# A two-part last output block, earlier loads on GpSimd and a shorter set-up, in a kernel of linear attention and an MLP

## The chip, the cores and the metric

The kernel runs on one core of a Trainium2 chip. The metric is the device time of one execution in microseconds (us). A profiled execution also gives a "span", from the core's first to its last instruction, some 2 us less than the time. Five engines run side by side: PE (TensorE), VectorE (DVE), ScalarE (ACT), GpSimd (POOL) and SyncE (SP).

## The reference, cut to what matters

```python
def _attn_ref(q, k, v, lam):            # q, k, v: 4 x 8 heads x 768 x 64
    for b in range(nb):                 # blocks of the sequence
        intra = einsum(qb, kb) * Dmask  # Dmask = lam ** (i - j) where i >= j, else 0
        intra = einsum(intra, vb)
        inter = einsum(qb * lam_pow, kv_state)
        out[:, :, sl] = intra + inter
        kv_state = lam_block * kv_state + einsum(kb_dec, vb)

def _moe_ref(x, w_in, w_out):           # x: 3072 x 512, made of the attention's output
    h = x @ w_in                        # 512 -> 2048
    g = np.where(h >= 1, h, np.where(h <= -1, 0.0, (h + 1) ** 2 / 4))
    return g @ w_out                    # 2048 -> 512
```

## The kernel before: the parts that matter

The tokens come in 24 chunks of 128. The decay is folded into q and k by tables of exponentials, made from a row of positions. A plan, computed when the kernel is built, gives each engine its order of work. The first six chunks are "plain" (transposed on PE through an identity matrix), and their loads, but for chunk 0's k and q, are issued by POOL, as are the weights, in four quarters each. I call the first product `h` L1 and the second L2.

```python
pos_i = const.tile([128, NCB], I32)
nc.gpsimd.iota(pos_i, pattern=[[C, NCB]], base=-S // 2, channel_multiplier=1)
row_i = const.tile([128, S], I32)                       # S = 768
nc.gpsimd.iota(row_i, pattern=[[1, S]], base=-S // 2, channel_multiplier=0)
ident = const.tile([128, 128], BF16)
make_identity(nc, ident)                                # two instructions on POOL
# ... cut ...
def tabq(i, hp):
    r = row[:, i * C:(i + 2) * C].rearrange("p (a b) -> p a b", b=C)
    nc.scalar.activation(out=tab_q[:, i:i + 2, hp, :], in_=r, func=AF.Exp, scale=ln_t[:, hp:hp + 1])
# ... cut ...
order = [("c", 0), ("c", 1), ("w", 0), ("c", 2), ("w", 1), ("c", 3), ...]    # chunks and weight quarters
# ... cut ...
def f_l2(s, ms, kg):                                    # one 128 x 512 block of the output, 16 products
    if kg == 0:
        py_t[s, ms] = pp_y.tile([128, d_model], F32, name="py", tag="py")
    for ko in range(4 * kg, 4 * kg + 4):
        nc.tensor.matmul(py_t[s, ms], lhsT=gT[s][:, ko, ms * 128:(ms + 1) * 128], rhs=w_out_sb[:, ko, :],
                         start=(ko == 0), stop=(ko == FO - 1))
def f_y(s, ms):
    osb[s, ms] = op.tile([128, d_model], F32, name="osb", tag="osb")
    nc.scalar.copy(out=osb[s, ms], in_=py_t[s, ms])
# ... cut ...
for _ in range(int((t - pe_end - 60) // (216 if t > 8000 else 430))):        # dummy matmuls where the plan sees PE wait
    nc.tensor.matmul(spin, lhsT=idle[:, 0:128], rhs=idle, start=True, stop=True)
```

## Time and profile before

| | before |
|---|---|
| time, median of three runs (lowest to highest) | 216.89 us (216.68 to 216.95) |
| time and span of the profiled execution | 215.84 and 213.8 us |
| first load issued by POOL | 2.17 us |
| first L1 matmul, second run of L1 | 13.12 and 18.29 us |
| last matmul ends, kernel ends | 209.88 and 213.82 us |

### The profile page before, as it was taken

How to read it: one execution, taken by the hardware profiler on the slowest of the kernel's cores; microseconds unless marked ns; L12 is line 12 of the kernel's file. 1: busy time of each engine (PE TensorE's matmuls, PEld its weight loads, DVE VectorE, ACT ScalarE, POOL GpSimd, SP SyncE). 2: the span in 40 equal slices, each digit the busy share in tenths (PEclk: the TensorE clock that was granted, in tenths of full speed). 3: DMA queues.
4: the chain of work that ended last, by engine and by line, in shares of the span. 5: the costliest groups of instructions: out<-in, count | busy, mean ns of one | idle time of the engine just before them, and what ended most of it. 6: DMA issues, size and time to landing. Idle time of an engine off the chain costs nothing.

```text
span 213.8 us, 5674 instructions
## 1 busy us (share of the span) xinstructions
PE 206.2 (96%) x2306; PEld 146.3 (68%) x2306; DVE 160.4 (75%) x238; ACT 150.6 (70%) x305; POOL 118.2 (55%) x150
## 2 busy tenths in 40 slices
PE   7899999999999999999899989999999999999992
PEld 2576988676759886978777767767776776666440
DVE  7627898989998999999999999779658546455100
ACT  6798785398668899699799778776778755444121
POOL 8999726169999799687477863865743000000000
PEclk9999999999999999999999999999999999999999
DMA  5999999999999998978977868888870310111121
GB/s 133 243 241 268 203 260 268 212 217 260 229 265 260 231 234 204 208 173 165 237 200 168 213 140 191 216 159 195 201 169 19 107 49 3 49 49 52 49 88 59
DMA packets 95593, 36.80 MB, mean 172 GB/s; under 512 B 87376, under 2 KB 91472, under 8 KB 95568
## 3 DMA queue, kind: packets, MB, share of 16 engines
q1 hardware_dynamic: 89920, 28.06, 58.0%
q0 software_dynamic: 5504, 8.39, 18.1%
q8 instruction: 18, 0.29, 0.6%
q14 instruction: 7, 0.06, 0.1%
q10 hardware_dynamic: 144, 0.00, 0.0%
HBM read 27.27 MB, written 6.29 MB: 157 GB/s over the span
## 4 chain that ended last, share of the span: by engine, by line
PE 64%; DVE 22%; POOL 5%; issue 3%; DMA 2%; ACT 2%; ACTq 0%; POOLq 0%
PE py L418 30%; PE ph L379 26%; DVE w L397 6%; DVE t L393 4%; DVE gT L412 4%; DVE kq L270 3%; DMA x2f<-in_v_dram 2%; DVE kq L267 2%; DVE sc L342 2%; POOL vn L281 1%; PE pu L318 1%; PE po L362 1%; PE ps L335 1%; PE po L360 1%; POOL x2f L461 1%
## 5 line engine op out<-in xcount | busy, mean ns | idle before, releaser
L379 PE MATMUL ph<-xT,w_in_sb 128*128 128x128 bf16 (+1 forms) x1152 | 97.2, 237 | 0.0
L418 PE MATMUL py<-w_out_sb,gT 128*128 128x512 bf16 x384 | 94.3, 379 | 0.0
L379 PEld LDWEIGHTS <-w_in_sb 128*128 128x128 bf16 x1152 | 80.2, 98 | 11.6 <-DMA w_in_sb<-in_moe_w_in_dram 0.4
L387 ACT ACTIVATE r<-ph,one 128x512 bf16<-128x512 f32 x96 | 65.0, 687 | 32.2 <-PE ph L379 20.3
L284 POOL TENSOR_TENSOR vn<-x2f,tab_k 64x256 bf16<-64x256 f32 x72 | 57.5, 798 | 32.3 <-DMA x2f<-in_v_dram 22.0
L418 PEld LDWEIGHTS <-gT 128*128 128x128 bf16 x384 | 35.2, 98 | 29.7
L393 DVE TENSOR_SCALAR t<-r 128x1024 bf16<-128x1024 bf16 x48 | 29.7, 620 | 19.8 <-ACT r L387 19.6
L412 DVE TENSOR_TENSOR gT<-w,t 128x1024 bf16<-128x1024 bf16 x48 | 39.5, 823 | 1.5
L397 DVE TENSOR_TENSOR w<-r,t 128x1024 bf16<-128x1024 bf16 x48 | 38.9, 811 | 1.2
L321 ACT CAST ubd<-pu 64x256 bf16<-64x256 f32 x76 | 27.7, 365 | 6.1 <-PE pu L318 5.2
L287 POOL COPY vi<-vn 64x512 bf16<-64x512 bf16 x36 | 30.6, 850 | 2.0
L423 ACT COPY osb<-py 128x512 f32<-128x512 f32 x24 | 14.0, 585 | 12.9 <-PE py L418 11.4
L265 ACT CAST kq<-x1f 64x256 bf16<-64x256 f32 x54 | 21.7, 401 | 0.6
L369 ACT CAST xT<-po 128x512 bf16<-128x512 f32 x24 | 14.0, 583 | 4.4 <-PE po L362 2.1
L270 DVE TENSOR_TENSOR kq<-x0f,tab_n 128x512 bf16<-128x512 f32 x18 | 15.1, 836 | 0.2
L342 DVE TENSOR_TENSOR sc<-ps,causal 128x512 bf16<-128x512 f32 x18 | 12.3, 682 | 3.4 <-PE ps L335 3.3
L235 PE MATMUL py<-idle 128*128 128x512 bf16 x34 | 11.5, 462 | 1.2 <-DVE one L120 1.2
L267 DVE TENSOR_TENSOR kq<-x1f 64x256 bf16<-64x256 f32 x18 | 11.7, 652 | 0.6
L362 PE MATMUL po<-sc,vi 128*128 128x64 bf16 x144 | 10.5, 193 | 1.6 <-DVE sc L342 1.5
L318 PEld LDWEIGHTS <-kq 128*128 128x128 bf16 x132 | 7.7, 98 | 4.6
L360 PEld LDWEIGHTS <-ubd 128*128 128x128 bf16 x132 | 8.9, 98 | 2.5 <-issue 1.7
L360 PE MATMUL po<-xq,ubd 128*128 128x64 bf16 x132 | 10.5, 193 | 0.0
(62 smaller groups left out, 127.5 us busy)
## 6 DMA issues: line engine op xcount, KB each, us to landing
out_dram<-osb SPq DMA_DIRECT2D x24, 256.0 KB, 2.3
x1f<-in_k_dram SPq DMA_DIRECT2D x19, 256.0 KB, 3.5
x0f<-in_q_dram SPq DMA_DIRECT2D x19, 256.0 KB, 4.0
x2f<-in_v_dram SPq DMA_DIRECT2D x18, 256.0 KB, 4.1
w_in_sb<-in_moe_w_in_dram POOLq DMA_DIRECT2D x4, 512.0 KB, 7.5
w_out_sb<-in_moe_w_out_dram POOLq DMA_DIRECT2D x4, 512.0 KB, 11.8
x2f<-in_v_dram POOLq DMA_DIRECT2D x6, 256.0 KB, 5.9
x1f<-in_k_dram POOLq DMA_DIRECT2D x5, 256.0 KB, 6.8
```

The costliest lines, as they stand in the source:

```text
L265: nc.scalar.copy(out=o, in_=i)
L270: nc.vector.tensor_tensor(kq[c % NKQ][:, 2 * HP:, :].rearrange("p a (b d) -> p (a b) d", b=2), qkv_ld[c, 0], _bc(tab_n[:, c % NCB, :], 2, ...
L284: nc.gpsimd.tensor_tensor(vn[c % NV][HD[hi], HP * g:HP * g + HP, :], quarter(qkv_ld[c, 2], g, hi), _bc(tab, 2, D), op=AX.mult)
L287: nc.gpsimd.tensor_copy(vi[c % NV][HD[hi], :, HD[hi]], vn[c % NV][HD[hi]])
L321: nc.scalar.copy(out=ubd[(2 * c + j) % NUB][HD[hi], :, HD[hi]], in_=pu[0][HD[hi], :, HD[hi] if c < NCB else HD[0]])
L360: nc.tensor.matmul(po[:, hp, HD[j]], lhsT=ubd[(2 * c + j - 1) % NUB][:, hp, :], rhs=qT[c][:, hp, HD[j]], start=True, stop=False)
L379: nc.tensor.matmul(ph[:, j * m:(j + 1) * m], lhsT=w_in_sb[:, ko, (i + j) * 128:(i + j + 1) * 128], rhs=xT[s][:, ko, p * m:(p + 1) * m], st ...
L387: nc.scalar.activation(out=r_t[grp][:, i, :], in_=ph_t[s, ni, part], func=AF.Relu, bias=one[:, 0:1])
L393: nc.vector.tensor_scalar(t_t[grp], r_t[grp], 0.5, 1.0, op0=AX.mult, op1=AX.min)
L397: nc.vector.tensor_tensor(w_t[grp], r_t[grp], t_t[grp], op=AX.subtract)
L412: nc.vector.tensor_tensor(o, w, t, op=AX.mult)
L418: nc.tensor.matmul(py_t[s, ms], lhsT=gT[s][:, ko, ms * 128:(ms + 1) * 128], rhs=w_out_sb[:, ko, :], start=(ko == 0), stop=(ko == FO - 1))
```

## The change

It has four parts. (1) Set-up: POOL makes a row of 256 positions, not 768; the identity moves to VectorE; the tables of later chunk pairs get their offset as a bias. So POOL's loads start sooner. (2) The plan is told that POOL is free at 1200 ns, not 2250, and orders anew. (3) `WIDE` goes from 4 to 6: the scores of chunks 4 and 5 are made in one step, into two banks. (4) The last output block is computed as 384 and then 128 columns, evicted by two engines and stored in two pieces.

```diff
-    PLAIN, KA, WIDE = 6, 2, 4
+    PLAIN, KA, WIDE = 6, 2, 6
+    CUT = 384
-    row_i = const.tile([128, S], I32)
-    nc.gpsimd.iota(row_i, pattern=[[1, S]], base=-S // 2, channel_multiplier=0)
+    row_i = const.tile([128, 2 * C], I32)
+    nc.gpsimd.iota(row_i, pattern=[[1, 2 * C]], base=-S // 2, channel_multiplier=0)
-    make_identity(nc, ident)
+    nc.vector.tensor_tensor(ident, row[:, 0:128], pos[:, 0:1].to_broadcast([128, 128]), op=AX.is_equal)
-    nc.scalar.copy(out=row[:, 2 * C:], in_=row_i[:, 2 * C:])
+        off = dict(bias=off_q[:, i // 2, hp:hp + 1]) if i else {}
+            nc.scalar.mul(off_q[:, i], ln_t, float(2 * C * i))
... (cut) ...
-            y = pst[c, 1] = wide
+            y = pst[c, 1] = wide if c < 4 else pp_t.tile([128, HP, 128], F32, name="pt", tag="pt")
-            add(("t", c), ..., [..., ("qT", c - 1)], ...)
+            add(("t", c), ..., [..., ("qT", c - 1), ("m", c - 1, 1) if c > 4 else None], ...)
... (cut) ...
+        parts = [(py_t[s, ms][0], slice(0, CUT if last else d_model), range(4 * kg, 4 * kg + 4))]
+        if last and kg == CPS - 1:
+            py_t[s, ms].append(pp_y.tile([128, d_model], F32, name="py", tag="py"))
+            parts.append((py_t[s, ms][1], slice(CUT, d_model), range(FO)))
... (cut) ...
+            nc.vector.tensor_copy(osb[s, ms, 1][:, n:], py_t[s, ms][1][:, n:])
... (cut) ...
-    run_plan({"PE": 5500, "ACT": 4450, "DVE": 4650, "POOL": 2250, "DMA": 2700, "SP": 800})
+    run_plan({"PE": 5500, "ACT": 4450, "DVE": 4650, "POOL": 1200, "DMA": 2700, "SP": 800})
```

More of the change, by code (lines that the diff above doesn't have):

```diff
@@ L5 @@
 from concourse import mybir
-from concourse.masks import make_identity
 from concourse._compat import with_exitstack
@@ L121 @@
     pos = const.tile([128, NCB], F32)
-    row = const.tile([128, S], F32)
+    row = const.tile([128, 2 * C], F32)
     nc.vector.tensor_copy(pos, pos_i)
-    nc.vector.tensor_copy(row[:, 0:2 * C], row_i[:, 0:2 * C])
+    nc.vector.tensor_copy(row, row_i)
+    nc.vector.tensor_tensor(ident, row[:, 0:128], pos[:, 0:1].to_broadcast([128, 128]), op=AX.is_equal)
     late = const.tile([128, 1], F32)
@@ L147, in tabq, with f_off @@
     def tabq(i, hp):
-        r = row[:, i * C:(i + 2) * C].rearrange("p (a b) -> p a b", b=C)
-        nc.scalar.activation(out=tab_q[:, i:i + 2, hp, :], in_=r, func=AF.Exp, scale=ln_t[:, hp:hp + 1])
-    const.tile([128, 8], F32, name="pad1")
+        off = dict(bias=off_q[:, i // 2, hp:hp + 1]) if i else {}
+        nc.scalar.activation(out=tab_q[:, i:i + 2, hp, :], in_=row.rearrange("p (a b) -> p a b", b=C), func=AF.Exp,
+                             scale=ln_t[:, hp:hp + 1], **off)
+    off_q = const.tile([128, NCB // 2, HP], F32)
+    def f_off():
+        for i in range(1, NCB // 2):
+            nc.scalar.mul(off_q[:, i], ln_t, float(2 * C * i))
+    const.tile([128, 52], F32, name="pad1")
     w_in_sb = big.tile([128, KO, d_ff], BF16)
@@ L414, in f_l2 @@
     def f_l2(s, ms, kg):
+        last = (s, ms) == (NST - 1, CPS - 1)
         if kg == 0:
-            py_t[s, ms] = pp_y.tile([128, d_model], F32, name="py", tag="py")
-        for ko in range(4 * kg, 4 * kg + 4):
-            nc.tensor.matmul(py_t[s, ms], lhsT=gT[s][:, ko, ms * 128:(ms + 1) * 128], rhs=w_out_sb[:, ko, :],
-                             start=(ko == 0), stop=(ko == FO - 1))
+            py_t[s, ms] = [pp_y.tile([128, d_model], F32, name="py", tag="py")]
+        parts = [(py_t[s, ms][0], slice(0, CUT if last else d_model), range(4 * kg, 4 * kg + 4))]
+        if last and kg == CPS - 1:
+            py_t[s, ms].append(pp_y.tile([128, d_model], F32, name="py", tag="py"))
+            parts.append((py_t[s, ms][1], slice(CUT, d_model), range(FO)))
+        for t, j, kos in parts:
+            for ko in kos:
+                nc.tensor.matmul(t[:, j], lhsT=gT[s][:, ko, ms * 128:(ms + 1) * 128], rhs=w_out_sb[:, ko, j],
+                                 start=(ko == 0), stop=(ko == FO - 1))
     def f_y(s, ms):
         osb[s, ms] = op.tile([128, d_model], F32, name="osb", tag="osb")
-        nc.scalar.copy(out=osb[s, ms], in_=py_t[s, ms])
+        n = CUT if len(py_t[s, ms]) > 1 else d_model
+        nc.scalar.copy(out=osb[s, ms][:, 0:n], in_=py_t[s, ms][0][:, 0:n])
+        if n < d_model:
+            osb[s, ms, 1] = op.tile([128, d_model], F32, name="osb", tag="osb")
+            nc.vector.tensor_copy(osb[s, ms, 1][:, n:], py_t[s, ms][1][:, n:])
     def f_st(s, ms):
         m0 = s * MS + ms * 128
-        nc.sync.dma_start(out=out[m0:m0 + 128, :], in_=osb[s, ms])
+        n = CUT if len(py_t[s, ms]) > 1 else d_model
+        nc.sync.dma_start(out=out[m0:m0 + 128, 0:n], in_=osb[s, ms][:, 0:n])
+        if n < d_model:
+            nc.sync.dma_start(out=out[m0:m0 + 128, n:], in_=osb[s, ms, 1][:, n:])
     T0, STEP, LEAD = 24000, 1000, 5000
@@ L498 @@
     add(("tabk",), "ACT", 250, lambda: nc.scalar.activation(out=tab_k, in_=arg, func=AF.Exp, scale=-1.0))
+    add(("off",), "ACT", 2 * 230, f_off, [("tab", 0, 3)])
     add(("tabn",), "ACT", 250, lambda: nc.scalar.activation(out=tab_n, in_=arg, func=AF.Exp), [("x", PLAIN - 3)])
@@ L510 @@
         for hp in range(HP) if P and c % 2 == 0 else ():
-            add(("tab", c, hp), "ACT", 410, lambda c=c, hp=hp: tabq(c, hp), [("tab", c, hp - 1), (None, ("kb", 0), ("x", 1))[c // 2]])
+            add(("tab", c, hp), "ACT", 410, lambda c=c, hp=hp: tabq(c, hp), [("tab", c, hp - 1), ("off",) if c else None, (None, ("kb", 0), ("x", 1))[c // 2]])
         free = [("xt", c - NKQ), ("u", c - NKQ, 0), ("u", c - NKQ, 1), ("zk", c % NKQ)]
@@ L526 @@
         if P:
-            add(("t", c), "PE", mm(*[128] * 8), lambda c=c: f_t(c), [("cast", c, 0), ("cast", c, 1), ("kb", c - 1), ("qT", c - 1)], due=od - 9000, extra=FILL)
+            add(("t", c), "PE", mm(*[128] * 8), lambda c=c: f_t(c), [("cast", c, 0), ("cast", c, 1), ("kb", c - 1), ("qT", c - 1), ("m", c - 1, 1) if c > 4 else None], due=od - 9000, extra=FILL)
             add(("kb", c), "ACT" if c < KA else "DVE", 590 if c < KA else 430, lambda c=c: f_kb(c), [("t", c), ("s", c - 2, 0), ("s", c - 2, 1)])
```

## The prediction

> **What bounds the kernel now.** I read the busy shares first, then the order-of-time chain of waits, then the engine timelines of the first 30 us and the last 10 us, then counts of matmuls by form in stretches of time.
>
> From the page of the kernel before (busy time, and the granted clock in 40 slices):
>
> ```profile
> span 213.8 us, 5674 instructions
> PE 206.2 (96%) x2306; PEld 146.3 (68%) x2306; DVE 160.4 (75%) x238; ACT 150.6 (70%) x305; POOL 118.2 (55%) x150
> ...
> PEclk9999999999999999999999999999999999999999
> DMA  5999999999999998978977868888870310111121
> ```
>
> PE is busy for 96% at full clock, but "busy" overlaps pipelined matmuls, so I counted instead. In the chain 16 matmuls of 128 columns take 0.89 us (55.6 ns each), 8 of 256 columns 0.87 us (109 ns), 4 of 512 columns 0.86 us (216 ns), one of 64 columns some 29 ns. The forms list has 768 + 184 useful ones of 128 columns, 384 of 256, 384 of 512 and 552 of 64: 52.9 + 41.9 + 82.9 + 16.0 = 193.7 us that no reordering removes. The same count by stretch gives: 18.3 to 209.9 us, 191.6 us long, 187.4 us of useful matmuls, 0.9 us of dummy ones (on the `idle` tile), 3.4 us of gaps (1.8 of them from 66 to 124, 0.8 from 24 to 66, 0.2 from 124 to 196). Before 18.3 us only some 6.5 us of useful work is done. So the span is a head of about 12 us, a TensorE stretch that is 98% full, and a tail of 3.9 us with nothing on PE. The long row of VectorE entries in the chain from 71 to 124 us is not where the time is lost: PE loses only 1.8 us there.
>
> The head, first the chain in order of time, then POOL's and VectorE's timelines:
>
> ```profile
> 0.92 0.76 POOL row_i L101
> 2.22 1.03 POOL x2f L461
> 3.25 0.88 POOL x1f L461
> ...
> 10.46 5.24 DMA x2f<-in_v_dram
> 15.78 1.05 POOL vn L281
> ```
> ```profile
> 0.92 0.76 POOL L101 IOTA row_i<- 128x768 int32 x1
> 1.63 0.22 POOL masks.py:197 MEMSET ident<- 128x128 bf16 x1
> 1.93 0.29 POOL masks.py:199 TENSOR_SCALAR_AFFINE_SELECT ident<-ident 128x128 bf16<-128x128 bf16 x1
> 2.17 1.08 POOL L461 DMA_DIRECT2D x2f<-in_v_dram  x1
> ...
> 6.64 1.07 POOL L281 TENSOR_TENSOR vn<-x2f,tab_k 128x512 bf16<-128x512 f32 x1
> ```
> ```profile
> 1.06 0.65 DVE L123 CAST pos<-pos_i 128x6 f32<-128x6 int32 x1
> ```
>
> See that POOL issues the loads of every chunk but the first, that three set-up instructions stand ahead of its first load, and that the chain runs through POOL's issues and a DMA until 15.7 us. From the second slice on the DMA engines are full (the 9s), in the first they are half free.
>
> The tail, from the timeline of the last 11 us:
>
> ```profile
> 202.81 7.07 PE L418 MATMUL py<-w_out_sb,gT 128*128 128x512 bf16 x32
> 209.96 0.58 ACT L423 COPY osb<-py 128x512 f32<-128x512 f32 x1 [2.87 <-PE py L418]
> ```
>
> The last matmul ends at 209.9, ScalarE evicts 128x512 until 210.54, SP's store is issued at 210.6, and the kernel ends at 213.8: 3.9 us in series.
>
> **What the Trainium skill says.** "SBUF — State Buffer", section "SBUF: two separate sides", says VectorE and GpSimd share a port pair as an exclusive lock for a whole instruction. The trace fits: the `pos` cast of 6 elements took 0.65 us and ended at 1.71, as the 768-column iota on POOL ended at 1.68. "Perfetto Trace Analysis", section "DMA Instruction — SWDGE (GPSIMD)", says a POOL DMA's duration is descriptor generation, not the move: the trace has 0.88 us on POOL but 3.8 us or more to landing, so an early start of the issue is what can be gained. "DMA: Bandwidth & Descriptors", section "Anatomy of one DMA — SWDGE (gpsimd) path", gives about 2.0 us fixed plus bytes for a transfer; the 256 KB stores here (issued by SP, another path) land in 2.0 at least and 2.3 us in the median, so a smaller last store gains little there. "TensorE: Matmul & The Clock Gate", section "Back-to-back issue gap", gives some 81 ns for sustained 128-column pairs; this trace shows 55.6, and I use 55.6.
>
> **The change part by part.**
>
> 1. Head, POOL. The row iota shrinks from 768 to 256 columns: 0.76 x 256/768 = 0.25 us. The two identity instructions go (POOL was on them from 1.68 to 2.22). First load: from 2.2 to about 0.92 + 0.28 = 1.2, 1.0 us earlier. The changed instruction order shows all of chunk 1 and 2's k and q and the first weight quarter ahead of the first `vn`: the issue of chunk 2's v moves from 10.46 to about 1.2 + 1.03 + 3 x 0.88 + 0.8 + 2 x 0.88 + 1.05 = 8.5. But the DMA engines are full from about 5 us on, so its landing, 15.7, is set by when the traffic began: I give it 1.0 us, not 2. The first `vn` goes from 6.64 to about 7.5; its matmuls are now behind the first scores, and the next consumer (the first attention output, 9.83) waits for VectorE's masked scores, so I count 0 for that.
>
> 2. Head, VectorE and ScalarE. Added on VectorE: the identity, 128x128 f32, as the equal `plain` compare takes 0.29 us. It starts earlier because the iota holds it up 0.5 us less; VectorE idles 0.64 us before 4.42 anyway, waiting for `lam`. Cost on the path: 0. ScalarE loses the 0.62 us row cast (it sat idle afterwards for `lam`, 0.63 us) and gains two multiplies of 128x4 at about 0.2 us before `tab_k` (5.89); ScalarE then waits 0.41 us for PE. Net 0 to +0.2.
>
> 3. Middle. `WIDE` 4 to 6: chunks 4 and 5 write both halves of the scores in one step, the second into the transposes' bank, so 16 matmuls of 128 columns stay 16 and the extra serial wait on VectorE goes; in return the transposes of chunk 5 wait for chunk 4's second mask. PE work is equal. The plan is recomputed, and the order on all engines moves from chunk 2 on; dummy matmuls go from 34 to 36 (0.4 us, where PE would have waited). With 3.4 us of gaps in 191.6 I expect -0.2, with a spread of 1 us either way.
>
> 4. Tail. The last block becomes 384 + 128 columns: 16 x (216 x 0.75 + 55.6) ns = 3.48 against 16 x 216 ns = 3.45 us: +0.03 to 0.05. ScalarE's 384-column copy (about 0.45 us) lies beside the last 0.89 us of PE. VectorE's 128x128 copy from PSUM: `plain` of that size took 0.29, against 0.58: -0.3. The last store has 64 instead of 256 KB: I take 0.2 off. The first store is issued about 0.4 us before PE ends, so it lands some 1.8 us after, before the second's 2.4. Sum -0.45.
>
> Sum: -1.0 + 0.1 - 0.2 - 0.45 = -1.55. 216.89 - 1.55 = 215.3 us.
>
> **Rivals.** (a) The head's gain is absorbed: DMA, full from 5 us on, lands chunk 2's v no earlier, or the early POOL loads crowd out SP's loads of chunk 0's k and q, which start the work at 4.63. For it: the row of 9s. Against: the first slice has half its DMA time free, and a backlog that starts sooner ends sooner. It would leave 216.3. (b) The new order opens gaps: VectorE from 66 to 124 is busy 56.2 of 58 us, and its bf16 operations last 1.00 instead of 0.69 us beside POOL; any order that puts a mask or `gT` late stalls PE. Against: PE had 1.8 us of loss there and work of two layers to choose from. It would take back 1 us or more: 216.3 to 217. (c) The new order closes gaps, by the wider scores and by weights that come earlier: at most 3.4 us are there, and I would expect 1 of them: 214.3. (d) The tail gains nothing since the 192 KB store ends last: +0.4, 215.7.
>
> **Range and chances.** Head -0.5 to -1.3, tail -0.2 to -0.8, middle -1 to +1: adding them loosely gives 213.9 to 216.6 for 8 in 10. Faster by over 2% would be under 212.6, more than head, tail and nearly every PE gap together: 0.04. Slower by over 2%, over 221.2, needs a new stall of some 6 us: 0.02. Within 2%: 0.94.
>
> **What would show it.** POOL's first load at about 1.2 us with a row iota of 0.25; the `pos` cast short; chunk 2's v landing at about 14.7 and its `vn` at about 14.8. From about 17 us on PE full, with useful matmuls counted by form leaving about 3 us of gaps. At the end a VectorE copy of 128x128 of 0.26 to 0.29 us and about 3.4 us from PE's last matmul to the end. The prediction is wrong if the first L379 run does not come about 1 us earlier than 13.1, if the stretch from 66 to 124 us shows more than 3 us of PE gaps, or if the time from the last matmul to the end stays 3.9.

## The result, and the profile after

The changed kernel took 213.78 us in the median of four runs (213.49 to 214.54), against 216.88 (before, with a fourth run): 3.1 us less. The ratio is 0.9864, with an interval of 0.9836 to 0.9892. Ratios here are the mean time of one kernel's runs over that of the other's in the same rounds, so not quite the ratio of the medians. Faster, but by less than 2%.

From the page of the kernel after:

```profile
span 212.4 us, 5710 instructions
PE 205.3 (97%) x2324; PEld 146.7 (69%) x2324; DVE 160.2 (75%) x240; ACT 150.4 (71%) x306; POOL 116.1 (55%) x148
...
DMA  5999999999999999894997969978861400110112
```

The profiled span shrank by 1.4 us only, less than half of what the timed runs show. The profiled execution of before was that kernel's fastest (215.84 us), this one the slowest of its four (214.54). So a comparison of these two traces alone misleads, and the head shows where. POOL's and then VectorE's timeline after (start, duration, engine, line, operation):

```profile
0.93 0.33 POOL L101 IOTA row_i<- 128x256 int32 x1
1.40 1.08 POOL L480 DMA_DIRECT2D x2f<-in_v_dram  x1
...
7.71 1.04 POOL L287 TENSOR_TENSOR vn<-x2f,tab_k 128x512 bf16<-128x512 f32 x1
8.69 0.93 POOL L480 DMA_DIRECT2D x2f<-in_v_dram  x1
```
```profile
1.06 0.23 DVE L122 CAST pos<-pos_i 128x6 f32<-128x6 int32 x1
1.29 0.29 DVE L123 CAST row<-row_i 128x256 f32<-128x256 int32 x1
1.62 0.29 DVE L124 TENSOR_TENSOR ident<-row,pos 128x128 bf16<-128x128 f32 x1
```

POOL's first load is 0.77 us earlier, and the position cast takes 0.23 us in place of 0.65 and ends at 1.29, again just after the iota (1.26). Yet the chain in order of time (start, duration, what) reaches the second run of L1 when it did before, 18.28 against 18.29:

```profile
2.48 4.58 DMA x1f<-in_k_dram
...
10.62 7.62 DMA w_in_sb<-in_moe_w_in_dram
18.24 0.05 issue
18.28 1.96 PE ph L385 x32
```

What PE waits for is the second quarter of `w_in`. It was issued 0.76 us earlier and landed at 18.24 us in both traces. So either earlier issues gain nothing, since the DMA engines are full, or one of the two traces is unusual.

The tail after, from the timeline of the last microseconds:

```profile
208.45 0.48 ACT L436 COPY osb<-py 128x384 f32<-128x384 f32 x1 [2.01 <-PE py L430]
208.95 0.33 SPq L444 DMA_DIRECT2D out_dram<-osb  x1
209.35 0.29 DVE L439 COPY osb<-py 128x128 f32<-128x128 f32 x1 [11.31 <-PE py L430]
209.67 0.33 SPq L446 DMA_DIRECT2D out_dram<-osb  x1
```

The larger part is evicted and on its way before PE ends; after PE's end (209.26) only 0.29 us of VectorE and the small store remain. It lands at 211.23. In both kernels the end comes 1.2 us after the last landing.

### The profile page after: what moved, and what is told of

Its sections match the earlier page's. It is cut to its first block, busy times and chain, and to the rows that moved or that the text cites. A ratio compares the mean times of both kernels' runs of the same rounds, so it can differ in the third digit from the quotient of the medians.

```text
span 212.4 us, 5710 instructions
## 1 busy us (share of the span) xinstructions
PE 205.3 (97%) x2324; PEld 146.7 (69%) x2324; DVE 160.2 (75%) x240; ACT 150.4 (71%) x306; POOL 116.1 (55%) x148
## 3 DMA queue, kind: packets, MB, share of 16 engines
q0 software_dynamic: 5504, 8.39, 18.3%
## 4 chain that ended last, share of the span: by engine, by line
PE 66%; DVE 21%; DMA 6%; issue 3%; POOL 2%; ACT 1%; POOLq 0%; DVEq 0%
PE ph L385 29%; PE py L430 29%; DVE w L403 5%; DVE gT L418 4%; DVE t L399 4%; DVE kq L276 4%; DMA w_in_sb<-in_moe_w_in_dram 4%; DVE kq L273 2%; DMA x1f<-in_k_dram 2%; DVE sc L348 2%; PE po L368 2%; PE pu L324 1%; PE po L366 1%; PE ps L341 1%; POOL vn L287 1%
## 5 line engine op out<-in xcount | busy, mean ns | idle before, releaser
L430 PE MATMUL py<-w_out_sb,gT 128*128 128x512 bf16 (+2 forms) x400 | 95.0, 371 | 0.0
L399 DVE TENSOR_SCALAR t<-r 128x1024 bf16<-128x1024 bf16 x48 | 28.8, 601 | 20.4 <-ACT r L393 20.1
L293 POOL COPY vi<-vn 64x512 bf16<-64x512 bf16 x36 | 29.7, 824 | 2.0
L436 ACT COPY osb<-py 128x512 f32<-128x512 f32 (+1 forms) x24 | 13.9, 580 | 13.5 <-PE py L430 12.8
L276 DVE TENSOR_TENSOR kq<-x0f,tab_n 128x512 bf16<-128x512 f32 x18 | 15.9, 883 | 0.3
L273 DVE TENSOR_TENSOR kq<-x1f 64x256 bf16<-64x256 f32 x18 | 11.1, 618 | 0.5
L368 PEld LDWEIGHTS <-vi 128*128 128x128 bf16 x144 | 9.1, 98 | 1.6 <-issue 0.6
```

The lines of the kernel that those rows point to most:

```text
L276: nc.vector.tensor_tensor(kq[c % NKQ][:, 2 * HP:, :].rearrange("p a (b d) -> p (a b) d", b=2), qkv_ld[c, 0], _bc(tab_n[:, c % NCB, :], 2, ...
L293: nc.gpsimd.tensor_copy(vi[c % NV][HD[hi], :, HD[hi]], vn[c % NV][HD[hi]])
L368: nc.tensor.matmul(po[:, hp, HD[j]], lhsT=vi[c % NV][:, HP * j + hp, :], rhs=sc_sb[c, 1][:, hp, HD[j]], start=(cb == 0 and j == 0), stop=True)
L399: nc.vector.tensor_scalar(t_t[grp], r_t[grp], 0.5, 1.0, op0=AX.mult, op1=AX.min)
L430: nc.tensor.matmul(t[:, j], lhsT=gT[s][:, ko, ms * 128:(ms + 1) * 128], rhs=w_out_sb[:, ko, j], start=(ko == 0), stop=(ko == FO - 1))
```

## The experiments

All theories need one measure that does not depend on the order of work. I use the time that PE **lacks** by a moment: that moment, less the useful matmuls done by then, each counted, once begun, as its columns / 2.4 + 2.3 ns (128 columns 55.6 ns, 512 columns 216 ns, as the prediction reads them from the chain). It counts dummies and gaps alike. Useful work is 193.6 us in every kernel. Worked out from each run's trace, with the landing of the second quarter of `w_in` (called quarter 1; issue plus time to landing):

| trace | quarter 1 lands | PE lacks by 24 us | lost from 24 us to the last matmul | last matmul to end |
|---|---|---|---|---|
| before | 18.24 | 12.65 | 3.63 | 3.94 |
| after | 18.24 | 12.65 | 2.97 | 3.15 |
| e1, before + last block | 19.32 | 13.76 | 3.05 | 3.13 |
| e2, before + set-up | 16.41 | 12.04 | 3.83 | 3.94 |
| e3, before + plan start | 19.19 | 14.38 | 3.87 | 3.94 |
| e4, before + wide | 19.13 | 13.60 | 3.15 | 3.95 |
| e5, after again | 17.32 | 12.21 | 2.39 | 3.13 |
| e6, after without last block | 18.17 | 12.60 | 2.69 | 3.95 |
| e7, after without wide | 17.84 | 12.26 | 4.17 | 3.13 |
| e8, after with old plan start | 17.25 | 12.04 | 3.01 | 3.14 |
| e9, after again | 17.37 | 12.15 | 3.15 | 3.13 |
| e10, after, POOL delayed | 20.62 | 15.04 | 3.76 | 3.13 |
| e11, after, v first | 17.88 | 12.54 | 3.16 | 3.13 |
| e12, after, one store | 18.75 | 13.15 | 2.75 | 3.72 |

Twelve kernels ran, each correct, each timed five rounds. e1 to e4 ran on one chip beside before at 217.37 us, e5 to e8 beside 217.36, e9 to e12 on another chip beside 217.58. My first theory was what the two traces say: the head gains nothing because the DMA engines are full (theory D), the tail gives 0.8 us (T), and the order in the middle the rest (O). The main rival was that of the prediction: the head's gain gets through (H).

**e1: the two-part last block alone.**

```diff
 (before)
+    CUT = 384
+    (the new f_l2, f_y and f_st)
```

> The kernel before with the two-part last block alone; every engine's order else unchanged. Theory T (what the two traces say: last matmul to end 3.9 before, 3.1 after): faster by 0.8 us, ratio 0.9963, and last matmul to end 3.1 us. Rival: the gain of 3.1 us in the timed runs is all from the order in the middle, and the two-part block gives 0.3 us or less.

Measured: 216.02 us, ratio 0.9946 (0.9909 to 0.9983). Last matmul to end: 3.13 us, as expected. The timed gain, 1.2 us in the ratio, has an interval from 0.4 to 2.0, so it does not contradict 0.8.

This run also told of the head. Its order up to the last block is that of before. PE's timeline (in brackets, the idle time ahead and what ended it):

```profile
14.48 1.96 PE L380 MATMUL ph<-xT,w_in_sb 128*128 128x128 bf16 x32 [1.39 <-DMA w_in_sb<-in_moe_w_in_dram]
19.36 1.96 PE L380 MATMUL ph<-xT,w_in_sb 128*128 128x128 bf16 x32
```

Here the first L1 run starts at 14.48 and the second at 19.36, over a microsecond later than in the first trace of before, and both behind weights.

**e2: the set-up alone.**

```diff
 (after)
-    PLAIN, KA, WIDE = 6, 2, 6  and the two-part block
+    PLAIN, KA, WIDE = 6, 2, 4  and one block, as before
-    run_plan({..., "POOL": 1200, ...})
+    run_plan({..., "POOL": 2250, ...})
```

> The set-up alone: short row iota, identity on VectorE, biases; the plan's start for POOL stays at 2250, so the order on all engines is nearly that of before. Theory D (DMA engines are full from 4 us on, so loads issued 0.8 us earlier land no earlier): 0 to -0.3 us, the second run of 32 L1 matmuls still starts near 18.3. Rival H (the head gain of my prediction gets through in the timed runs): -0.8 to -1.3 us.

Measured: 215.70 us, ratio 0.9926 (0.9885 to 0.9967), that is 1.6 us less, interval 0.7 to 2.5. Theory D falls. The quarter landed at 16.41 here, 1.3 us before the run of L1 that needs it; by then that run waited behind other work. The second L1 run, in PE's timeline:

```profile
17.71 1.95 PE L384 MATMUL ph<-xT,w_in_sb 128*128 128x128 bf16 x32
```

**e3: the plan's start alone.**

```diff
 (before)
-    run_plan({..., "POOL": 2250, ...})
+    run_plan({..., "POOL": 1200, ...})
```

> The kernel before with the plan's POOL start 1200 in place of 2250 and nothing else: only the order on the engines changes. Theory O (the order in the middle carries what the tail does not): -1 to -2 us. Rival: order is noise, within 0.5 us either way.

Measured: 217.89 us, ratio 1.0021 (0.9989 to 1.0053): no gain, so theory O falls too, in the form that the new order alone gains. The trace shows a loss in the head that I had not expected. First PE's timeline, then busy time by stretch (each row ends with the granted clock, the DMA share and GB/s):

```profile
8.65 0.38 PE L318 MATMUL pu<-vn,c 128*128 128x128 bf16 x4 [1.78 <-POOL vn L281]
```
```profile
8.00:10.00 2.00, 1.35 (x15) 0.74 (x15) 0.60 (x1) 1.43 (x3) 2.00 (x3) 0.89 0.87 130
10.00:12.00 2.00, 2.00 (x17) 1.20 (x17) 1.26 (x3) 1.00 (x3) 1.99 (x3) 0.50 1.19 199
12.00:14.00 2.00, 2.00 (x21) 0.92 (x18) 0.79 (x3) 1.60 (x4) 2.00 (x4) 0.76 0.96 261
```

The plan now believes that POOL is free a microsecond sooner than it is, and puts one more load ahead of the first `vn` (7.53 us against 6.64). PE stands idle for 1.78 us, and its clock is halved from 9.56 to 12.98 us. Of the six executions five show a granted clock of 0.989 to 0.992 in the mean and the fastest (217.43 us) 1.0, so the halving comes with most executions, not with all. With the long set-up the early start costs; whether it helps with the short one, e8 asks.

**e4: the wide scores alone.**

```diff
 (before)
-    PLAIN, KA, WIDE = 6, 2, 4
+    PLAIN, KA, WIDE = 6, 2, 6
+    (second half of the scores of chunks 4 and 5 into the transposes' bank, and the wait for it)
```

> The kernel before with both halves of the scores of chunks 4 and 5 in one step and the new wait of the transposes, nothing else. Theory W (the saved serial wait is what shortens the middle): -0.5 to -1.5 us, fewer PE gaps from 24 to 66 us. Rival: 0 within 0.3 us.

Measured: 216.57 us, ratio 0.9962 (0.9927 to 0.9998), a gain between 0 and 1.6 us. Its trace loses 3.15 us after 24 us, inside the 3.05 to 3.83 of the traces with before's order (before, e1, e2). Not settled by this run. Two things are to be known of it. The plan is made anew, so beside the wide step the order of work changes on all engines (on PE from its 386th useful matmul on). And the expected place was missed: from 24 to 66 us PE loses 2.1 us here, against 1.1 in before; what is won comes later.

**e5: the changed kernel again.** No edit.

> The changed kernel again, for a second trace and as the mark of the three runs beside it. Theory S (the parts add: tail -0.8 from the trace, set-up -1.0 to -1.6, wide scores with the new order about -0.5): ratio 0.986 to 0.989, about 3 us under before; time that PE lacks by 24 us in this trace 11.5 to 12.3 us instead of 12.65. Rival: the first trace was typical, 12.65 by 24 us, and the gain is later.

Measured: 213.96 us, ratio 0.9847 (0.9820 to 0.9873). The quarter landed at 17.32, and PE lacked 12.21 us by 24 us: theory S (the parts add, though the ratio is a little below the 0.986 that it gave), and the first trace of after was a slow one in the head. PE's timeline:

```profile
17.77 1.95 PE L385 MATMUL ph<-xT,w_in_sb 128*128 128x128 bf16 x32
```

**e6: without the last block.**

```diff
 (after)
-    CUT = 384
-    (the new f_l2, f_y and f_st)
+    (those of before)
```

> The changed kernel without the two-part last block. Theory T: 0.8 us slower than the changed kernel (ratio to before 0.990 where that has 0.986), last matmul to end 3.9 us. Rival: 1.2 us or more, as the timed run of the block alone had it (1.17, interval 0.4 to 2).

Measured: 215.02 us, ratio 0.9889 (0.9861 to 0.9917), so 1.1 us over e5, of which the head of this run may hold some. The tail in the trace is 3.95 us: the block is worth 0.8 us there.

**e7: without the wide scores.**

```diff
 (after)
-    PLAIN, KA, WIDE = 6, 2, 6
+    PLAIN, KA, WIDE = 6, 2, 4
-    (the second bank and its wait)
```

> The changed kernel with the scores of chunks 4 and 5 in two steps again. Theory W: 0.5 to 1 us slower than the changed kernel, and PE lacks that more between 24 and 66 us. Rival: the order that the plan makes of it is chance, within 0.3 us.

Measured: 214.95 us, ratio 0.9893 (0.9867 to 0.9918), 1.0 us over e5. The trace loses 4.17 us from 24 us on, where e5 loses 2.39; 2.9 of it falls between 40 and 66 us, where e5 loses about 0.5. Who waited for whom on PE (total, times, longest), first in this run from 36 to 66 us, then in e5 from 24 to 124 us:

```profile
PE po L368 <- DVE sc L348: 1.6, 1, 1.6
PE ph L385 <- ACT xT L375: 0.7, 1, 0.7
```
```profile
PE po L368 <- DVE sc L348: 1.0, 1, 1.0
```

In this order PE waits 1.6 us for a masked score tile of VectorE, already in the first 66 us. So the wide scores go with the new order: they win back what it would lose there. e5 gives a part of that back later (1.7 us lost after 66 us against 0.6 here), which is why 2.4 us there became 1.8 in total and 1.0 in the timed runs. This run too was planned anew: but for the set-up and the last block, its order on PE is that of e3, as that of e8 below is that of e4. So there are four plans, and the table above gives what each loses from 24 us on, in the mean:

| plan | narrow scores | wide scores |
|---|---|---|
| POOL from 2250 | 3.5 (before, e1, e2) | 3.1 (e4, e8) |
| POOL from 1200 | 4.0 (e3, e7) | 2.9 (after, e5, e6, e9, e11, e12) |

The wide scores are worth about 0.4 and 1.2 us there. (e10 has the last plan too and lost 3.8, but its head was disturbed, so it is left out.) No run parts the wide step itself from the new order that it brings.

**e8: the old plan start.**

```diff
 (after)
-    run_plan({..., "POOL": 1200, ...})
+    run_plan({..., "POOL": 2250, ...})
```

> The changed kernel with the plan's POOL start of before, 2250: same instructions, other order. The order alone cost 0.5 us in the kernel before (interval -0.2 to 1.1). Theory P (the start has to agree with where POOL really is: the plan then puts loads ahead of the first product): slower than the changed kernel by 0.5 us or more. Rival: equal or faster, the start was no help.

Measured: 214.40 us, ratio 0.9869 (0.9839 to 0.9899), 0.4 us over e5 with overlapping intervals. Whether the new start helps the changed kernel stays open: the two intervals together allow from -0.4 to 1.3 us (an estimate). In the head it looks like a cost: PE lacks 12.04 us by 24 us in both traces with the new set-up and the old start (e2, e8), and 12.15 to 13.15 in the six with the new start (after, e5, e6, e7, e9, e12).

**e9: the changed kernel as a mark.** No edit.

> The changed kernel once more, as the mark of the three runs beside it on this chip, and for a third trace: ratio to before 0.984 to 0.987, the second weight quarter lands at 17.2 to 18.3 us.

Measured: 214.53 us, ratio 0.9865 (0.9841 to 0.9888); quarter at 17.37 us.

**e10: POOL delayed.** This turns the disputed cause up.

```diff
 (after)
     ident = const.tile([128, 128], BF16)
+    scratch = const.tile([128, S], I32)
+    for i in range(2):
+        nc.gpsimd.iota(scratch, pattern=[[1, S]], base=i, channel_multiplier=0)
```

> The changed kernel with two more iotas of 768 columns on POOL ahead of its first load: first load at about 2.8 instead of 1.4 us, the order on all engines unchanged. Theory H (the head is set by when POOL's loads begin, since the DMA engines work off a queue): about 1.3 us slower than the mark, second weight quarter 1.3 us later. Rival D (the DMA engines are full anyway, so POOL's start does not matter): within 0.3 us of the mark, quarter lands where it did.

Measured: 216.49 us, ratio 0.9951 (0.9918 to 0.9983), 2.0 us over the mark. POOL's timeline, and PE's second L1 run:

```profile
1.22 1.60 POOL L105 IOTA scratch<- 128x768 int32 x2
2.76 1.08 POOL L483 DMA_DIRECT2D x2f<-in_v_dram  x1
```
```profile
20.66 1.51 PE L388 MATMUL ph<-xT,w_in_sb 128*128 128x128 bf16 x24 [1.36 <-DMA w_in_sb<-in_moe_w_in_dram]
```

Loads that begin 1.37 us later end in a quarter that lands some 3 us later in this trace, and in 2.0 us of time. Theory H holds. Whether the delay costs more than one for one is not shown: the intervals of this run and the mark together allow some 1.0 to 2.7 us (an estimate), and the profiled execution was the slowest of its six (217.39 us). A part of the loss comes early: PE lacked 9.1 us by 10 us against 8.3, waiting 1.66 us for the first `vn`. The iotas also held VectorE's row cast up (0.84 us in place of 0.29), but by 4.42 us VectorE was where it was in the changed kernel (4.47). The scratch tile also moves later buffers by 3072 bytes; I take that as harmless, but no run shows it.

**e11: the first load ahead of the iotas.** A try at a better kernel.

```diff
 (after)
+    v00 = ld.tile([128, H, D], F32, name="x2f", tag="x2f")
+    nc.gpsimd.dma_start(out=v00, in_=v[0][:, 0:C, :].rearrange("h p d -> p h d"))
     pos_i = const.tile([128, NCB], I32)
     (VectorE's four clears of ubd moved ahead of its casts)
```

> The changed kernel with the first load of v issued before both iotas (and VectorE's four clears ahead of its casts): first load at about 0.84 instead of 1.40 us, the later loads where they were. Theory H, if what counts is the first load: -0.3 to -0.5 us against the mark. Rival: the later loads are what counts, or loads of k and q by SP are crowded out: 0 within 0.3 us, or slower.

Measured: 214.95 us, ratio 0.9882 (0.9853 to 0.9911): 0.4 us over the mark, a miss. POOL's timeline:

```profile
1.27 1.08 POOL L99 DMA_DIRECT2D x2f<-in_v_dram  x1 [0.82 <-POOLq L616]
...
2.81 0.91 POOL L485 DMA_DIRECT2D x1f<-in_k_dram  x1
```

The load went out at 1.27, not at 0.84, so it won 0.1 us, and all later loads left 0.35 us later (2.81 against 2.47). The quarter landed 0.5 us later than in the mark. SP's loads of chunk 0's k and q landed later too, at 4.96 and 5.85 us (4.68 and 5.58 in the mark), and the first products with them, which is the other rival of the expectation. So the first load alone wins nothing; which of the two cost more is not shown. The times' intervals overlap, and the quarter varies by more than 0.5 us between traces of one kernel.

**e12: one store for the last block.**

```diff
 (after)
-    (two tiles, two stores of 192 and 64 KB)
+    (one tile, one store of 256 KB once both copies are done)
```

> The changed kernel with both parts of the last block in one tile and one store of 256 KB in place of 192 and 64 KB; the two-part product and its evictions stay. In the traces a last store of 256 KB takes 2.02 us to land and one of 64 KB 1.56: slower than the mark by 0.46 us, last matmul to end 3.6 us. Rival: the early store of the larger part is what matters, or the timed difference of the whole block (1.1 to 1.2 us) is mostly this: 0.8 us or more.

Measured: 214.78 us, ratio 0.9869 (0.9836 to 0.9901), 0.25 us over the mark and within its interval (the ratios differ by 0.0004 only). The trace is clearer: 3.72 us from last matmul to end against 3.13. The stores at the end (KB each, us to landing), first in before, then the two of after:

```profile
out_dram<-osb SPq DMA_DIRECT2D x1, 256.0 KB, 2.0
```
```profile
out_dram<-osb SPq DMA_DIRECT2D x1, 192.0 KB, 1.9
out_dram<-osb SPq DMA_DIRECT2D x1, 64.0 KB, 1.6
```

To two digits 2.02, 1.88 and 1.56 us. So of the tail's 0.8 us, 0.29 are the shorter copy and 0.46 the smaller last store.

## Why the prediction was right or wrong

The call (within 2%) was right, but it was wide: it would have held from 212.6 to 221.2 us. The time lay just outside the range, 213.78 us, a hair under the low end of 213.9, and just inside it when run again, 213.96 and 214.53 us. The predicted gain of 1.55 us was half of the measured 3.1. The mechanisms of the head and the tail were right; in the traces two terms of the sum, the middle and the tail, were too small, and a part of the timed gain can't be placed.

- **"What bounds the kernel now."** Right: a head, a full TensorE stretch, and a tail. Useful work stayed at 193.6 us, and everything gained came from time that PE lacked. Two readings were off, and neither enters the sum: POOL issues the loads of the first six chunks only (SP has 18 of the 24 chunks), and by 18.3 us 6.3 us of useful work are done, not 6.5.
- **Step 1, the head, "I give it 1.0 us".** The mechanism is right: POOL's first load was 0.77 us earlier (not 1.0: the short iota took 0.33 us, not 0.25), e2 took 1.6 us off and e10 put 2.0 on. The load named was not the whole of it. Chunk 2's v, foretold for 14.7 us, landed at 15.18 in after and at 14.88 in e5; but where the second weight quarter lands late, it is the quarter that ends the wait: the second run of L1 starts 0.04 to 0.05 us after it in before, after, e1, e6, e7, e10 and e12. Where it lands early (e2, e5, e8, e9), that run starts at 17.70 to 17.77, 0.4 to 1.3 us after it, so that a still earlier quarter would gain nothing there. In size, the mean of PE's lack by 24 us is 13.3 us in the traces with before's order in the head (before, e1, e4) and 12.5 in the six with that of the changed kernel (after, e5, e6, e7, e9, e12): 0.8 us, where the prediction had 0.9 with step 2. (e3 is left out, since its stall is in neither kernel; with the old start, in e2 and e8, it is 12.0.) That the quarter should come 1.3 us earlier in the mean (18.97 us in before, e1, e3 and e4, 17.67 in after, e2, e5 to e9 and e12) for issues 0.76 earlier is not explained by the issue alone; what the rest is stays open.
- **"The first vn ... I count 0."** About right: by 10 us PE lacks 0.2 us more than before (8.33 against 8.11), by 13 us 0.1 more (9.77 against 9.66).
- **Step 2.** Right on the path: `tab_k` moved from 5.89 to 6.13 us, and ScalarE's next copy still came earlier, 6.26 against 6.53, so the 0.1 us of cost in the sum does not show. One cost was overlooked: an exponential with a bias takes 593 ns in the mean against 492 without, eight times. ScalarE was busy for 71% of the span.
- **Step 3, the middle, "I expect -0.2, with a spread of 1 us either way".** Too small. From 24 us to the last matmul, before's order loses 3.5 us in the mean (before, e1, e2), the new one 2.9 (after, e5, e6, e9, e11, e12): 0.6 us. The instruction order had shown that the middle moves, not which way. The wide scores carry it, together with the new order (the four plans at e7). Rival (b) named the right engine: PE waits for a mask of VectorE in the middle of before (0.81 and 0.73 us), of e5 (1.03) and most of all of e7 (1.58), there ending at 65.5 us, just before the stretch that it named.
- **Step 4, the tail.** Right in kind, and rival (d) was wrong: the 192 KB store landed at 210.83 us, the small one at 211.23. The mis-sized term is "the last store ... I take 0.2 off": it was 0.46. Sum 0.8 instead of 0.45.
- **Rival (a)** looked proven by the first two traces and fell in e2 and e10. The test that I had written, the first L1 run a microsecond before 13.1, was a bad one: it starts at 13.1 to 14.5 with the old set-up (before, e1, e4) and at 13.2 in after and e5, since it hangs on one landing that varies by a microsecond and more.

The three terms as the traces have them, 0.8, 0.6 and 0.8, make 2.2 of the 3.1 us. The rest is about what luck in the profiled executions can hide: those of before, e1 and e4 were 0.65 us faster than the timed medians of their kernels in the mean, those of after, e5, e6, e7, e9 and e12 0.1 us slower (an estimate from the times of each run). In which stage that part lies, no trace says; e2's timed gain, 0.7 to 2.5 us, leaves room for it in the head. That the two first traces showed only 1.4 us is the same scatter at its worst, a lucky trace of before beside an unlucky one of after.

## What to carry to other kernels

Before you explain a change from two traces, look where their executions lie among the timed ones, and trace kernels that share the disputed part; experiments for other questions give such traces for nothing. Where loads queue for full DMA engines, what stands ahead of the first load can still count: here two iotas more, 1.37 us, cost 2.0 us (e10). Check a planner's model of when an engine is free against the trace: the start time of 1200 ns cost a stall, and in most executions a halved clock, with the long set-up (e3), and no gain of it is shown with the short one (e8).

## What the Trainium skill lacked or had wrong

- "TensorE: Matmul & The Clock Gate", section "HAM oscillation — how this bites in real kernels", has the rule that PE should have no idle gaps over some 3.4 us. In e3 the longest gap in that stretch was 1.78 us, among short work, and the clock was halved for 3.4 us (9.56 to 12.98). With gaps of 0.5 us there (after) it stayed at 1.0, but so it did with gaps of 1.66 us in e10 (to 10.16 us) and 1.84 us in e4 (to 61.93 us): in these runs the length of one gap does not decide it.
- The same page, section "Back-to-back issue gap", gives some 81 ns for sustained matmuls of 128 columns with their weight loads; 16 of them took 0.89 us here, 55.6 ns each, which is the section's figure of some 56 ns for a single one.
- "DMA: Bandwidth & Descriptors", section "Anatomy of one DMA — SWDGE (gpsimd) path", gives a fixed 2.0 us and bytes / 436 GB/s for POOL's path; no page that I read gives such a sum for SP's. Stores issued by SP landed in 1.56, 1.88 and 2.02 us for 64, 192 and 256 KB, so a fixed part of about 1.4 us (an estimate, from the line through the first and last). The slope is that of the page: 192 KB less make 0.45 us by its rate (an estimate from the page's figure) and 0.46 us here. So the prediction's "gains little there" was its own step, and the page's rate would have given the tail's missing part.
- No page that I read gives the cost of an iota: 0.13, 0.33 and 0.76 us for 6, 256 and 768 columns on 128 partitions. None gives how early POOL's first DMA can go out: 1.27 us in e11, though none of the kernel's own lines stood ahead of it, where an iota starts at 0.84.
